# A new order for the opening, two sums of squares in two parts, g_norm loaded later, one cast behind a copy

## The chip, the core and the metric

The kernel runs on one core of a Trainium2 chip. The metric is the device time of one execution in microseconds; a verdict compares the medians of several executions. TensorE is PE, with its weight loads as PEld; VectorE is DVE, ScalarE is ACT, GpSimd is POOL, and SyncE is SP, which issues most of the DMAs.

## The reference

Linear attention without softmax, an RMS norm over each head, then two layers over 4608 tokens of 512 numbers, all in float32:

```python
kv = np.einsum('bhsd,bhse->bhde', k, v)            # 8 batches, 8 heads, 576 x 64
out = np.einsum('bhsd,bhde->bhse', q, kv)
rms = np.sqrt(np.mean(out * out, axis=-1, keepdims=True) + 1e-06)
x = out / rms * g_norm                              # -> 4608 tokens x 512
h = x @ w_in                                        # 2048
x = (np.maximum(h, 0) + np.log1p(np.exp(-np.abs(h)))) @ w_out
h = np.maximum(np.maximum(x @ w1, x @ w2), x @ w3)  # 768
y = h @ w_out2
```

## The kernel before

Tokens lie along the free dimension, and are worked on in five passes of 2 x 456 or 2 x 464. A float32 product is made of three float32r products (high part with high, high with low, low with high), so each operand of the layers is split in two: a cast to the high part, and a subtraction for the low part. Passes 1 to 4 multiply 2 x 2 blocks in Strassen's way with seven products (numbered 1 to 7 in the code); pass 0 multiplies plainly, while the weights arrive, are converted, split and written back to DRAM for the later passes.

The opening is the work ahead of and at the start of pass 0. It is written out as a list, `OPENING`, of steps with indices and an option (an engine a, v or p for ACT, DVE, POOL, or a PSUM tag X, Y, W, at, cv). Eight pairs of heads, numbered 0 to 7 (four pairs for each of two halves of 456 tokens), go through it. For pair k: `LP.k` loads k, v and q on the SP queue (v of pairs 0 to 2 on ACT's), `mm.k` makes k^T v (the first with some idle products, `warm`, between), `ev.k` copies it out of PSUM, `o.k` multiplies q by it, `sq.k` squares the result on ACT, `ss.k` sums the squares over a head with a product by a block of ones, `rs.k` makes the root, `t.k`, `r1.k`, `r2.k`, `r3.k` refine and scale it (r1 uses g_norm as `gcol0`), `xh.k` and `xl.k` split the result. For the weights, `LW.g.i` loads raw numbers, `ra`, `rb` (ACT) and `ja`, `jb` (DVE) convert them, `wc` and `wl` split them, `s1` to `s4` and `cc`, `cl` make and split the sums for the later passes, and `SA`, `SB`, `SC` write parts back. `H.g.i.k` is a plain product of twelve matmuls for half k of the tokens; it needs four split pairs (0 to 3 for k = 0, 4 to 7 for k = 1), the split block `wl.g.i` and a free PSUM bank, and `sp`, `hc`, `hl` take it out through softplus and split it. After the list come the products for g = 8 and 9 (called Xx, Yx in the rows).

What sets the order: for times below `PIN` every engine issues its instructions in the order of the list (`pinned` queues each behind the last one of its engine), so an instruction that waits holds up everything behind it on that engine. The PSUM tags have 2 banks for X, Y and at, and 1 for W and cv. A bank of `o.k` is free after `r1.k`, one of `ss.k` after `r2.k`, one of `H` after `hl`. `load_gain` loads g_norm with a DMA on the SP queue and scales it with two DVE instructions; it is queued at `OPEN - 38.7`, ahead of the list. Raw loads of the weights that follow the list are tied to the last steps `jb` (`before` keeps their times).

In the passes 1 to 4, `combine` makes and splits the inputs of the seven products; its steps 1, 3, 4, 5 make those of products 5 and 6, 7, 4 and 3. `combine_x2` does it for the second layer's results, whose products (`run_group`, bank X for products 1, 6, 7, 4) follow; `sums` copies bank X out on ACT after products 1, 6 and 7 (`copy`). A product that goes on in bank X waits for that copy.

Of the kernel before, what the change touches and what calls it, by code (L numbers as in the profile page):

```python
# [9 lines left out]
F32R = mybir.dt.float32r  # L10
# [5 lines left out]
B, H, S, D = 8, 8, 576, 64  # L16
# [47 lines left out]
BANK = {1: "X", 6: "X", 7: "X", 4: "X", 5: "Y", 3: "Y", 2: "W"}

# [2 lines left out]
def kernel(  # L68
# [12 lines left out]
    nc = tc.nc  # L81
# [23 lines left out]
    def psum(tag, name):  # L105
        return ps.tile([P, 512], F32, tag=tag, bufs=PS_BUFS[tag], name=name)
# [4 lines left out]
    def ctile(name, n, dtype=F32):  # L111
        return wide(cp, "c", 10, name, n, dtype)
# [67 lines left out]
    def at(t, fn, *args):  # L180
        events.append((t, len(events), fn, args))
# [286 lines left out]
    qs, o_t, sq_t, ss_t, og_t, ra_t = {}, {}, {}, {}, {}, {}  # L468
# [118 lines left out]
    def square32(a, n, p):  # L587
# [126 lines left out]
    def run_pass(pas, base):  # L714
# [37 lines left out]
        start = {name: base + 7 * i for i, name in enumerate(order)}  # L752
# [43 lines left out]
        for fp in range(8):  # L796
            t = start[f"H{fp}"]
# [19 lines left out]
        for n in range(4):  # L817
            if pas == 0:
                for q in range(2):
                    t = start[f"X{n}{q}"]  # L820
# [10 lines left out]
            for q in range(2):  # L831
                t = start[f"X{n}{q}"]
# [150 lines left out]
        t = base3 + 2.05  # L983
# [42 lines left out]
    by = {"a": nc.scalar, "v": nc.vector, "p": nc.gpsimd}  # L1026
# [18 lines left out]
    def low(eng, hi, lo, src):  # L1045
        sub(eng, lo, src, hi.bitcast(F32))
# [14 lines left out]
    def pair(f):  # L1061
        return lambda k, *opt: f(k // NP * n0, n0, k % NP, *opt)
# [4 lines left out]
    def plus(g, i, k):  # L1067
# [162 lines left out]
```

## Time and profile before

| | |
|---|---|
| time, median of 3 runs (1357.93 to 1359.16) | 1359.15 us |
| the profiled execution, its own time | 1356.8 us |
| its span | 1355.0 us |
| PE busy | 1346.9 us (99%) |
| PEld busy | 1197.5 us (88%) |
| DVE, ACT, POOL busy | 821.7, 734.9, 650.2 us |

The profiled execution took 1.8 us more than its span, and 2.35 us less than the median. In the rows below, a time at the left is the start in us from the start of the span, and the next number is how long the instruction, or a run of like ones (x4), took. Brackets tell how long the engine's queue idled before it, and what ended that. L12 is line 12 of the kernel. A float32 matmul shows as two instructions, a float32r one as one; each has one weight load.

### The profile page before, as it was taken

The numbers are of one execution on the slowest core, as the hardware profiler recorded it, in microseconds if no ns is written. First come the engines' busy times: TensorE is split into PE (matmuls) and PEld (weight loads), VectorE is DVE, ScalarE is ACT, GpSimd is POOL, SyncE is SP. The second block draws the span as 40 slices with busy tenths as digits, with TensorE's granted clock in tenths as the row PEclk, the third lists the DMA queues.
The fourth block names the chain that finished last, engine by engine and source line by source line (L and its number), as shares of the span: only waits on it lengthen the run. The fifth ranks groups of instructions, "written<-read, shape, count | busy, mean of one in ns | idle before, by whom it ended". The sixth has DMA issues, their size and how long they took to land.

```text
span 1355.0 us, 20402 instructions
## 1 busy us (share of the span) xinstructions
PE 1346.9 (99%) x6956; PEld 1197.5 (88%) x6956; DVE 821.7 (61%) x1301; ACT 734.9 (54%) x1426; POOL 650.2 (48%) x612
## 2 busy tenths in 40 slices
PE   9999999999999999999999999999999999999998
PEld 6889999999888888888888888888888889998897
DVE  6856758883555767734556676445667754457444
ACT  6776657773755366446444664554356546443332
POOL 6866545665645635345335344444434444336320
PEclk9999999999999999999999999999999999999999
DMA  8799789777999686586678756766766576675765
GB/s 297 243 326 347 261 299 346 255 255 260 319 333 319 230 318 220 182 314 204 211 236 273 244 190 209 270 208 208 247 196 215 166 282 219 216 217 187 228 199 172
DMA packets 135543, 336.12 MB, mean 248 GB/s; under 512 B 14608, under 2 KB 41104, under 8 KB 135440
## 3 DMA queue, kind: packets, MB, share of 16 engines
q1 hardware_dynamic: 134864, 333.90, 74.1%
q8 instruction: 56, 0.92, 0.3%
q10 hardware_dynamic: 576, 0.92, 0.2%
q14 instruction: 47, 0.39, 0.1%
HBM read 269.35 MB, written 65.40 MB: 247 GB/s over the span
## 4 chain that ended last, share of the span: by engine, by line
PE 96%; DMA 2%; ACT 1%; DVE 1%; issue 0%; SPq 0%; ACTq 0%; DVEq 0%
PE Xo L155 6%; PE Xo L157 6%; PE Xo L156 6%; PE Xx L157 5%; PE Xx L155 5%; PE Xx L156 5%; PE Xh L155 5%; PE Xh L157 5%; PE Xh L156 5%; PE Yo L155 3%; PE Yo L156 3%; PE Yo L157 3%; PE Yx L155 3%; PE Yx L156 3%; PE Yx L157 3%; PE Yh L155 3%
## 5 line engine op out<-in xcount | busy, mean ns | idle before, releaser
L145 POOL TENSOR_TENSOR lo<-e,hi 128x464 fp32r<-128x464 f32 (+1 forms) x160 | 188.4, 1211 | 176.0 <-ACT hi L139 169.1
L139 ACT CAST hi<-t 128x464 fp32r<-128x464 f32 (+1 forms) x120 | 65.6, 546 | 125.2 <-DVE e L151 55.4
L155 PE MATMUL Xo<-hi,u 128*128 128x464 f32 (+1 forms) x296 | 110.8, 375 | 0.5 <-ACT m L139 0.4
L156 PE MATMUL Xo<-lo,u 128*128 128x464 f32 (+1 forms) x296 | 109.8, 371 | 0.0
L157 PE MATMUL Xo<-hi,u 128*128 128x464 f32 (+1 forms) x296 | 109.7, 371 | 0.0
L155 PE MATMUL Xh<-hi,u 128*128 128x464 f32 (+1 forms) x266 | 99.3, 373 | 1.0 <-DVE lo L151 0.9
L148 DVE TENSOR_TENSOR x<-x,Xx 128x464 f32<-128x464 f32 (+1 forms) x104 | 65.5, 632 | 56.2 <-PE Xx L157 55.8
L157 PE MATMUL Xh<-hi,u 128*128 128x464 f32 (+1 forms) x266 | 98.8, 371 | 0.0
L156 PE MATMUL Xh<-lo,u 128*128 128x464 f32 (+1 forms) x266 | 98.6, 371 | 0.0
L139 ACT CAST hi<-e 128x464 fp32r<-128x464 f32 (+1 forms) x160 | 86.0, 581 | 20.5 <-PE Yx L156 17.1
L139 ACT COPY m<-Xo 128x464 f32<-128x464 f32 (+1 forms) x108 | 58.5, 547 | 69.7 <-PE Xo L157 67.2
L145 DVE TENSOR_TENSOR lo<-t,hi 128x464 fp32r<-128x464 f32 (+1 forms) x120 | 75.8, 636 | 32.5 <-ACT hi L139 30.1
L155 PE MATMUL Xx<-hi,u 128*128 128x464 f32 (+1 forms) x256 | 95.2, 372 | 0.0
L157 PE MATMUL Xx<-hi,u 128*128 128x464 f32 (+1 forms) x256 | 95.0, 371 | 0.0
L156 PE MATMUL Xx<-lo,u 128*128 128x464 f32 (+1 forms) x256 | 94.8, 370 | 0.0
L151 POOL TENSOR_TENSOR e<-e 128x464 f32<-128x464 f32 (+1 forms) x32 | 38.1, 1190 | 106.9 <-DVE t L151 89.6
L145 POOL TENSOR_TENSOR lo<-m,hi 128x464 fp32r<-128x464 f32 (+1 forms) x40 | 47.8, 1212 | 74.4 <-ACT hi L139 74.4
L145 POOL TENSOR_TENSOR u<-sw,u 128x256 fp32r<-128x256 f32 (+1 forms) x67 | 67.5, 1022 | 33.0 <-ACT u L139 31.2
L139 ACT CAST u<-sw 128x512 fp32r<-128x512 f32 (+1 forms) x120 | 63.0, 541 | 35.6 <-POOL sw L151 17.9
L151 POOL TENSOR_TENSOR sw<-sw 128x256 f32<-128x256 f32 x84 | 66.5, 794 | 23.5 <-DVE sw L280 19.3
L148 DVE TENSOR_TENSOR Wh<-h,Wh 128x464 f32<-128x464 f32 (+1 forms) x32 | 20.6, 644 | 92.6 <-PE Wh L157 77.6
L663 POOL TENSOR_TENSOR og<-og,r 128x464 f32<-128x464 f32 (+1 forms) x32 | 40.4, 1262 | 69.5 <-DVE r L659 42.8
(260 smaller groups left out, 4102.8 us busy)
## 6 DMA issues: line engine op xcount, KB each, us to landing
u<-wd SPq DMA_DIRECT2D x241, 512.0 KB, 4.6
ux<-wd SPq DMA_DIRECT2D x99, 512.0 KB, 3.6
wd<-u SPq DMA_DIRECT2D x161, 256.0 KB, 4.8
u<-wd SPq DMA_DIRECT2D x104, 256.0 KB, 4.1
raw<-in_w_out_dram SPq DMA_DIRECT2D x22, 512.0 KB, 4.7
raw<-in_w_dram SPq DMA_DIRECT2D x18, 512.0 KB, 5.4
raw<-in_w_in_dram SPq DMA_DIRECT2D x16, 512.0 KB, 5.5
wd<-ahead SPq DMA_DIRECT2D x32, 256.0 KB, 5.8
```

Of the source, the lines that this page charges most:

```text
L139: nc.scalar.copy(hi, src)
L145: eng_lo.tensor_tensor(out=lo, in0=src, in1=hi.bitcast(F32), op=ALU.subtract)
L148: eng.tensor_tensor(out=o, in0=a, in1=b, op=ALU.add)
L151: eng.tensor_tensor(out=o, in0=a, in1=b, op=ALU.subtract)
L155: nc.tensor.matmul(acc, wh, xh, start=first, stop=False, skip_group_check=on)
L156: nc.tensor.matmul(acc, wh, xl, start=False, stop=False, skip_group_check=on)
L157: nc.tensor.matmul(acc, wl, xh, start=False, stop=last, skip_group_check=on)
L663: nc.gpsimd.tensor_tensor(out=og, in0=og, in1=r, op=ALU.mult)
```

## The change

- `OPENING` is a new list of the same steps with another order, other engines and other PSUM tags, and with four steps more: `vh.0`, `vl.0`, `vh.1`, `vl.1`, all on POOL. They split the squares of the pairs 0 and 1 into a high and a low float32r part, and `ss.0` and `ss.1` then take two float32r products with `ones` in place of a float32 one with `ones32`.
- `load_gain` is queued at `OPEN + 0.6`, between `LP.2` (`OPEN + 0.5`) and `mm.0` (`OPEN + 0.75`), on SP and on DVE.
- In the passes 2 and 3, for the second half of the columns, step 5 of `combine_x2` (the input of product 3) is traced 3.01 after the products' base time in place of 3.5 before it, with an order edge behind the ACT instruction traced last, which is the copy after product 6.

```diff
--- before.py
+++ after.py
@@ -43,23 +43,24 @@
 ENGINES = tuple(getattr(mybir.EngineType, e) for e in ("PE", "Activation", "DVE", "Pool", "SP"))
 LEAD = 10
 OPENING = """
-LP.0 LP.1 LP.2 mm.0 ev.0:a o.0:X LW.0.0 mm.1 sq.0 LP.3 ss.0:Y ev.1:a o.1:X rs.0 mm.2 r1.0 t.0:p sq.1 LP.4
-ra.0.0:cv ss.1:Y ev.2:v rb.0.0 r2.0 o.2:X rs.1 ja.0.0 mm.3 LP.5 sq.2 t.1:p r3.0 ss.2:Y ev.3:a r1.1 xh.0 o.3:W
-LP.6 jb.0.0 rs.2 xl.0:p mm.4 sq.3 r2.1 t.2:a r1.2 wc.0.0:p ss.3:Y ev.4:a r2.2 wl.0.0:p mm.5 LW.0.1 rs.3 r3.1
-o.4:X ev.5:a t.3:p LP.7 r1.3 xh.1 o.5:X r3.2 sq.4 xl.1:p mm.6 sq.5 r2.3 xh.2 ss.5:Y ev.6:v rb.0.1 xl.2:p r3.3
-ss.4:Y ra.0.1:cv LW.1.0 o.6:W rs.5 ja.0.1 xh.3 mm.7 t.5:p r1.5 LW.1.1 sq.6 jb.0.1 xl.3:p rs.4 r2.5 LW.2.0 ev.7:a
-r1.4 o.7:X ra.1.0:cv t.4:p r3.5 rb.1.0 ss.6:Y wc.0.1:p sq.7 H.0.0.0:X r2.4 s1.0 rs.6 ja.1.0 ra.1.1:at t.6:p r1.6
-ra.2.0:at wl.0.1:p jb.1.0 cc.0.1:a ss.7:Y rb.2.0 r2.6 LW.2.1 SA.0 wc.1.0:a cl.0.1 ja.2.0 H.0.1.0:Y rs.7 r3.4
-wl.1.0:p xh.5 SB.0 t.7:a jb.2.0 SC.0.1 xh.4 r2.7 LW.8.0 tab wc.2.0:p r1.7 H.1.0.0:Y r3.6 SA.1 ra.2.1:cv wl.2.0:p
-r3.7 sp.0.0.0 xh.6 xl.5:v hc.0.0.0:a xl.4:p H.2.0.0:X xh.7 hl.0.0.0 rb.2.1 xl.7:p s2.0 s3.0 SA.2 xl.6:v sp.0.1.0
-rb.8.0 ja.2.1 s4.0 H.0.0.1:X hc.0.1.0:a jb.2.1 sp.2.0.0 cc.0.2:p rb.1.1 hl.0.1.0 cl.0.2 LW.8.1 hc.2.0.0:a ja.1.1
-H.2.0.1:Y ra.8.0:cv hl.2.0.0 cc.0.0:p sp.0.0.1 ja.8.0 SC.0.2 cl.0.0 sp.1.0.0 jb.1.1 LW.9.0 hc.0.0.1:a hc.1.0.0:v
-ra.8.1:at s1.1 H.1.0.1:X jb.8.0 LW.9.1 wc.1.1:a cc.1.1:a hl.1.0.0 wl.1.1:p SC.0.0 sp.2.0.1 hl.0.0.1 rb.8.1
-cl.1.1 H.0.1.1:X hc.2.0.1:a ja.8.1 sp.1.0.1 s2.1 hl.2.0.1 wc.2.1:a SB.1 jb.8.1 s3.1 hc.1.0.1:a SC.1.1 wl.2.1:v
-wc.8.1:a H.1.1.1:Y s4.1 cc.1.0:a wl.8.1:v sp.0.1.1 cl.1.0 cc.1.2:a hl.1.0.1 hc.0.1.1:a SB.2 cl.1.2 s1.2 s2.2
-s3.2 s4.2 s1.8 s2.8 s3.8 s4.8 H.2.1.0:X hl.0.1.1 sp.1.1.1 SB.8 hc.1.1.1:v SC.1.0 hl.1.1.1 H.1.1.0:X SC.1.2
-sp.2.1.0 ra.9.0:cv rb.9.0 hc.2.1.0:v hl.2.1.0 ja.9.0 jb.9.0 H.2.1.1:X sp.1.1.0 ra.9.1:W wc.8.0:a hc.1.1.0:v
-hl.1.1.0 wl.8.0:v sp.2.1.1 rb.9.1 hc.2.1.1:v hl.2.1.1 ja.9.1 jb.9.1 SA.8
+LP.0 LP.1 LP.2 mm.0 ev.0:v mm.1 LW.0.0 o.0:X ev.1:v LP.3 o.1:X sq.0 mm.2 vh.0:p sq.1 vl.0:p LP.4 rb.0.0 ev.2:a
+vh.1:p ss.0:Y ra.0.0:cv o.2:W vl.1:p rs.0 ja.0.0 LP.5 mm.3 t.0:a r1.0 sq.2 r2.0 ss.1:Y ev.3:a jb.0.0 ss.2:Y rs.1
+LP.6 r3.0 wc.0.0:a o.3:X t.1:a wl.0.0:p r1.1 mm.4 rs.2 r2.1 sq.3 LW.0.1 mm.5 r1.2 t.2:a ss.3:Y ev.4:v xh.0 LP.7
+r3.1 ev.5:a xl.0:p o.4:X rs.3 r2.2 xh.1 o.5:W t.3:p r1.3 sq.4 SA.0 mm.6 r3.2 ra.0.1:cv xl.1:p sq.5 ss.4:Y LW.1.0
+r2.3 xh.2 mm.7 ev.6:v rb.0.1 xl.2:p r3.3 LW.1.1 rs.4 ss.5:Y ev.7:a ja.0.1 t.4:p o.6:X xh.3 r1.4 rs.5 xl.3:p
+o.7:at jb.0.1 ra.1.0:at r1.5 rb.1.0 LW.2.0 s1.0 H.0.0.0:X r2.4 ra.1.1:cv wc.0.1:p ja.1.0 cc.0.1:a t.5:p sq.6
+r3.4 sq.7 cl.0.1 ss.6:Y rb.1.1 jb.1.0 wl.0.1:p xh.4 r2.5 LW.2.1 rs.6 ja.1.1 ss.7:Y ra.2.0:at wc.1.0:p r1.6
+SC.0.1 t.6:a xl.4:p jb.1.1 H.0.1.0:X rs.7 SB.0 r2.6 wc.1.1:a wl.1.0:p LW.8.0 r1.7 t.7:a tab r3.6 wl.1.1:p
+H.1.0.0:Y r3.5 xh.6 SA.1 s1.1 sp.0.0.0 r2.7 xh.5 xl.6:p r3.7 cc.1.1:a SB.1 H.1.1.0:Y hc.0.0.0:a xh.7 xl.5:p
+hl.0.0.0 sp.0.1.0 xl.7:v sp.1.0.0 s2.1 ra.2.1:cv hc.0.1.0:v H.0.1.1:X cl.1.1 hc.1.0.0:a hl.0.1.0 rb.2.0 s3.1
+hl.1.0.0 rb.8.0 ja.2.0 s2.0 rb.2.1 SC.1.1 H.0.0.1:X jb.2.0 s4.1 cc.1.0:a ja.2.1 LW.8.1 sp.0.1.1 cl.1.0 cc.1.2:a
+jb.2.1 ra.8.0:at hc.0.1.1:v LW.9.0 H.1.1.1:Y cl.1.2 sp.1.1.0 ja.8.0 wc.2.0:a s3.0 hl.0.1.1 sp.0.0.1 SC.1.0 s1.2
+hc.1.1.0:a wl.2.0:v ra.8.1:cv s4.0 H.1.0.1:X SC.1.2 hl.1.1.0 rb.8.1 cc.0.0:p jb.8.0 rb.9.0 cl.0.0 SA.2 ja.8.1
+cc.0.2:a hc.0.0.1:a jb.8.1 H.2.0.0:Y sp.1.1.1 wc.2.1:p LW.9.1 hl.0.0.1 wc.8.1:a s1.8 wl.2.1:v sp.1.0.1 cl.0.2
+SC.0.0 hc.1.1.1:a wl.8.1:v hc.1.0.1:a H.2.0.1:X s2.2 sp.2.0.0 hl.1.0.1 s2.8 ra.9.0:cv SB.2 hl.1.1.1 s3.2
+ra.9.1:at SC.0.2 ja.9.0 hc.2.0.0:a s3.8 SB.8 H.2.1.0:X jb.9.0 rb.9.1 s4.2 sp.2.0.1 hl.2.0.0 s4.8 hc.2.0.1:a
+ja.9.1 wc.8.0:p hl.2.0.1 H.2.1.1:Y sp.2.1.0 wl.8.0:p jb.9.1 hc.2.1.0:v hl.2.1.0 sp.2.1.1 SA.8 hc.2.1.1:v
+hl.2.1.1
 """.split()
 BANK = {1: "X", 6: "X", 7: "X", 4: "X", 5: "Y", 3: "Y", 2: "W"}
 
@@ -590,7 +591,21 @@
         nc.scalar.activation(sq_t[a, p], o, AF.Square)
         og_t[a, p] = o
 
+    def square_hi(a, n, p, eng):
+        sh = ctile("sh", n, F32R)
+        cast(eng, sh, sq_t[a, p])
+        sq_t[a, p] = (sq_t[a, p], sh)
+
+    def square_lo(a, n, p, eng):
+        sq, sh = sq_t[a, p]
+        sl = ctile("sl", n, F32R)
+        low(eng, sh, sl, sq)
+        sq_t[a, p] = (sh, sl)
+
     def ssq_mm32(a, n, p, tag):
+        if isinstance(sq_t[a, p], tuple):
+            ssq_mm(a, n, p, tag)
+            return
         ss_t[a, p] = psum(tag, "ss")[:, 0:n]
         nc.tensor.matmul(ss_t[a, p], ones32, sq_t.pop((a, p)), start=True, stop=True)
 
@@ -852,10 +867,18 @@
         def combine_x2(q, steps):
             combine(xc_tile, R2, q, [x2[q, w] for w in TILES], steps, "at", (1, 2) if q else ())
 
+        def combine_behind(q, steps):
+            traced = reversed(nc.cur_bb.bb.instructions)
+            with tc.issue_after(next(i for i in traced if i.engine is mybir.EngineType.Activation)):
+                combine_x2(q, steps)
+
         for q in range(2 if pas else 0):
             for s, m in ((0, 2), (2, 4)):
                 at(start[f"X3{q}"] + SLOT[m] + 0.45, combine_x2, q, (s,))
-            at(start[f"X3{q}"] + (12.5, 10.5)[q], combine_x2, q, (1, 3, 4, 5))
+            late = q and pas in (2, 3)
+            at(start[f"X3{q}"] + (12.5, 10.5)[q], combine_x2, q, (1, 3, 4) if late else (1, 3, 4, 5))
+            if late:
+                at(start[f"X3{q}"] + 17.01, combine_behind, q, (5,))
         mx, R3 = {}, {}
 
         def h2_done(fp, j, w, src):
@@ -1011,7 +1034,7 @@
     def first_table():
         tables.update(set=NORM_SET, load=nc.scalar.preload_act_table_set(NORM_SET).ins)
 
-    at(OPEN - 38.7, load_gain)
+    at(OPEN + 0.6, load_gain)
     at(OPEN - 38.6, first_table)
     for b in range(2):
         at(OPEN - 50, kv_zero, b)
@@ -1074,6 +1097,8 @@
         "ev": lambda k, eng: kv_evict32(*divmod(k, NP), by[eng]),
         "o": pair(out_mm32),
         "sq": pair(square32),
+        "vh": pair(lambda a, n, p, eng: square_hi(a, n, p, by[eng])),
+        "vl": pair(lambda a, n, p, eng: square_lo(a, n, p, by[eng])),
         "ss": pair(ssq_mm32),
         "rs": pair(root),
         "t": pair(lambda a, n, p, eng: root_square(a, n, p, by[eng])),
```

## Rows read from the trace of the kernel before

**Rows 1.** Window: PE, PEld, DVE, ACT, POOL busy; clock, DMA share, GB/s

```profile
16.00:27.00 11.00, 10.70 (x107) 6.69 (x105) 9.66 (x16) 9.57 (x22) 9.44 (x9) 1.00 0.86 327
```

**Rows 2.** Timeline of PE, the start of the opening

```profile
2.04 2.93 PE L554 MATMUL warm<-kv 128*128 128x128 f32 x12 [2.04 <-DVE kv L535]
4.76 1.06 PE L545 MATMUL kvps<-v,k 128*128 128x128 f32 x4
...
7.59 1.03 PE L584 MATMUL o<-qraw,kv 128*128 128x456 f32 x2
8.55 0.95 PE L513 MATMUL kvps<-v,k 128*64 128x64 f32 x20
9.43 1.03 PE L595 MATMUL ss<-sq,ones 128*128 128x456 f32 x2
10.29 0.93 PE L584 MATMUL o<-qraw,kv 128*128 128x456 f32 x2
```

**Rows 3.** Timeline of PEld (weight loads), the H products and what follows

```profile
30.57 0.19 PEld L155 LDWEIGHTS Yh<-hi,u 128*128 128x128 f32 x1 [0.56 <-DVE t L618]
...
33.62 0.19 PEld L155 LDWEIGHTS Yh<-hi,u 128*128 128x128 f32 x1 [0.66 <-DVE t L618]
...
41.57 0.19 PEld L155 LDWEIGHTS Yh<-hi,u 128*128 128x128 f32 x1 [0.61 <-DVE lo L151]
41.68 0.19 PEld L156 LDWEIGHTS Yh<-lo,u 128*128 128x128 f32 x1
...
46.93 0.19 PEld L155 LDWEIGHTS Xh<-hi,u 128*128 128x128 f32 x1 [0.53 <-DVE lo L151]
...
53.06 0.19 PEld L155 LDWEIGHTS Xh<-hi,u 128*128 128x128 f32 x1 [1.27 <-ACT u L139]
...
60.45 0.19 PEld L155 LDWEIGHTS Xx<-hi,u 128*128 128x128 f32 x1
...
71.27 0.19 PEld L157 LDWEIGHTS Xx<-hi,u 128*128 128x128 f32 x1 [0.43 <-DVE u L145]
```

**Rows 4.** Timeline of SP, the DMA issue behind pair 2

```profile
6.60 0.33 SPq L257 DMA_DIRECT2D raw<-in_w_in_dram  x1
```

**Rows 5.** Waits of SP, 0:10 us: total, times, longest

```profile
SPq L257 <- DMA qraw<-in_qt_dram: 1.7, 1, 1.7
```

**Rows 6.** DMA issues, 0:14 us: count, KB, median us to landing

```profile
qraw<-in_qt_dram SPq DMA_DIRECT2D x6, 228.0 KB, 5.3
...
raw<-in_w_in_dram SPq DMA_DIRECT2D x1, 512.0 KB, 5.0
...
gcol<-in_gn_dram SPq DMA_DIRECT2D x1, 0.5 KB, 2.2
```

**Rows 7.** Timeline of DVE, g_norm's scaling and a copy out of PSUM

```profile
3.00 0.15 DVE L1008 TENSOR_SCALAR gcol<-gcol 128x1 f32<-128x1 f32 x1 [1.02 <-DMA gcol<-in_gn_dram]
...
12.15 0.46 DVE L141 COPY kv<-kvps 64x64 f32<-64x64 f32 x2 [0.22 <-PE kvps L513]
```

**Rows 8.** POOL by line and form, 7:62: count, busy us, mean ns

```profile
L151 POOL TENSOR_TENSOR lo<-og,hi 128x456 fp32r<-128x456 f32 x6 | 7.7, 1276 | 2.2 <-ACT hi L139 2.1
...
L141 POOL CAST u<-sw 128x512 fp32r<-128x512 f32 x4 | 2.9, 712 | 0.0
```

**Rows 9.** Timeline of ACT in pass 2, around the copies of Xo

```profile
735.57 0.58 ACT L139 CAST hi<-x 128x464 fp32r<-128x464 f32 x1
736.18 0.55 ACT L139 COPY m<-Xo 128x464 f32<-128x464 f32 x1
```

**Rows 10.** Timeline of PEld, second layer, passes 2 and 3

```profile
736.77 0.19 PEld L155 LDWEIGHTS Xo<-hi,u 128*128 128x128 f32 x1 [0.50 <-ACT m L139]
...
742.46 0.19 PEld L155 LDWEIGHTS Yo<-hi,u 128*128 128x128 f32 x1
...
999.78 0.19 PEld L155 LDWEIGHTS Xo<-hi,u 128*128 128x128 f32 x1 [0.29 <-ACT m L139]
```

**Rows 11.** Timeline of POOL in pass 2, low parts of the inputs

```profile
734.14 3.47 POOL L145 TENSOR_TENSOR lo<-x,hi 128x464 fp32r<-128x464 f32 x3 [1.13 <-ACT hi L139]
```


## The prediction

> **What bounds the kernel now.** I read the busy shares first: PE is busy 99% of the span, so only time in which PE's stream stands still can be won, and it has to be looked for in the weight loads, since matmul ends are modelled. A float32r product of 456 columns takes 0.207 us from load to load ((60.45 - 53.06 + 0.1) / 36 for three H products in a row), and where a load waits, the brackets show it; the load after it follows 0.11 instead of 0.21 later, so a bracket costs PE its figure less about 0.11 [rows 3]. From 30.57 to 60.45 four brackets cost 0.55 + 0.50 + 0.42 + 1.16 = 2.6, and one at 71.27 costs 0.3 [rows 3]. Behind that only two more carry anything: 0.50 in pass 2 and 0.29 in pass 3, both on ACT's copy of bank X [rows 10].
>
> Ahead of 30.57 there is hardly a gap: per pair, o takes 0.86 to 0.96, mm 0.88 and the float32 sum 0.86 [rows 2]. From the first o (7.59) to the product at 30.57 are 22.98 us; in them lie 8 o (8 x 0.87), 7 mm (7 x 0.88), 8 sums (8 x 0.86) and one H (12 x 0.207), together 22.5. The start is bound by PE, with DVE just behind it (9.66 busy of 11 us from 16 to 27, ACT 9.57, POOL 9.44) [rows 1].
>
> **Sums in two parts.** A float32 sum of 0.86 becomes two products of 0.207: -0.45 each, -0.9 for two. The price is two POOL steps before each sum: a cast (0.71 for 512 columns in the nearest row) and a subtraction (1.28) [rows 8]. Four of them are 4.0 us of POOL, at a time when nothing else is in its list. For pair 1 other products cover the latency; for pair 0 they do not: PE has only o.1 and mm.2 between o.0 and ss.0 (0.86 + 0.88 = 1.74), against a square on ACT (taken as the 0.58 of a like cast [rows 9]), cast and subtraction, 0.58 + 0.71 + 1.28 and some 0.2 for handing over = 2.77. PE waits 1.0 (0.3 if the cast takes 0.4 and the subtraction 1.0; 1.5 if both are a fifth longer).
>
> **g_norm later.** The one issue that SP saves at the head (0.33 for a load [rows 4]) moves no product, since the first ones follow the idle ones without a gap. What it is moved behind decides. On SP it now stands where the raw weights' load stood; that one waited 1.7 us for an earlier q to land and was issued at 6.60 [rows 4, 5]. On DVE its two scalings (0.15 each [rows 7]) now stand ahead of ev.0 and ev.1, which the new list gives to DVE, and behind these stand ja.0.0 and r1.0. So o.0 waits for g_norm, which it doesn't use. When does g_norm land? Alone it took 2.2 us; in this stretch a q of 228 KB takes 5.3, and the raw load of 512 KB, issued at 6.60, took 5.0 [rows 6]. Transfers land in the order of issue: 512 KB at about 400 GB/s are 1.3 us, so the raw load's turn came at 11.6 - 1.3 = 10.3. That is where I put g_norm: 10.3, with bounds 6.2 + 2.2 = 8.4 (issued 0.4 earlier, and not held up) and 11.0. I take 10.3, as the raw load had the very same place in the queue. Then 0.35 for the scalings, 0.46 for the copy [rows 7], 0.1 for handing over: o.0 starts at 11.2. PE, which now makes mm.1 first (7.59 to 8.47), waits 2.7 (bounds 0.9 and 3.4).
>
> **The rest of the new list.** To the second H product (H.0.1.0) PE has 22.5 - 0.9 of work, 2.7 + 1.0 of the waits above, and a wait of 1.0 near the end: ss.7 needs the Y bank that r2.5 frees, which hangs on t.5, fourth in a row of POOL steps, and H.0.1.0 the X bank that r1.6 frees. DVE, nearly full, starts its conversions and refinements only once g_norm is there (bounds 0 and 1.6, against 0.5 in all now). 7.59 + 21.6 + 3.7 + 1.0 = 33.9, where it was 30.57. The other way round the old waits behind it go: they are DVE's and ACT's, each 0.4 to 1.2 long, and PE arrives 3.3 later while DVE's work moves by less; the new list also makes the g = 2 products last, and reuses a bank only after two other products. 33.9 + 11 x 2.48 = 61.2, against 60.45: **+0.8** (bounds: -1.4 with the low ends of the waits, +2.0 with the high ones and 0.5 of waits left).
>
> The wait at 71.27 is for a block whose conversion queues behind a raw load tied to the last jb steps. In the old list jb.9.1 is DVE's last step; in the new one four DVE steps come after it, so these loads leave some 2 to 4 us sooner. That wait goes: **-0.3** (0 to -0.4). SA.0 now stands ahead of LW.1.0 on SP: 512 KB, 1.3 us later for LW.1.0 and LW.1.1. H.1.0.0 comes 2.5 us after H.0.1.0, which covers it; without that cover it costs up to 1.0, within the bounds.
>
> **The cast behind the copy.** In pass 2 the cast of product 3's input (735.57, 0.58) runs directly ahead of the copy of Xo (736.18 to 736.73), and PE's load comes at 736.77 [rows 9, 10]. With the cast behind the copy, the copy starts about 0.6 sooner, more than PE's loss of 0.50 - 0.11; the same in pass 3, 0.29 - 0.11. The moved cast delays its low part on POOL, the last of three up to 737.61 [rows 11], by some 0.4; the next product into Yo comes at 742.46 [rows 10], so that is covered. **-0.6** (bounds +0.2, if the cast then delays a later copy, and -0.8).
>
> **Sum.** +0.8 - 0.3 - 0.6 = -0.1 on the profiled execution's span of 1355.0 (1356.8 with what lies around it). Its time lies 2.35 below the median of the runs, so I set the change against the median: 1359.15 - 0.1, forecast 1359.0. A measurement of this kernel tells about 0.2%, 2.7 us, from no change: the forecast is the same.
>
> **Rivals.** (1) DVE isn't held by g_norm, because it lands early, about 8.4. Against it stands every landing in this stretch at 4 to 5 us after issue. Of the 2.7 not waited only some 1.2 come back, since DVE's 9.66 of 11 is the next bound: 1357.8. (2) The list does all it could: the front costs no more than pair 0's 1.0, no wait is left behind it, 0.5 + 2.6 + 0.3 of old waits go, the sums give 0.9 and the copies 0.6: -3.9, and so 1355.2. For it: 3.4 of waits are really there to be won. Against it: DVE's load, and g_norm. [...] (4) The cast isn't late, or ACT orders otherwise, so that passes 2 and 3 give nothing: 1359.6.
>
> **How the numbers follow.** Forecast 0.57, rival 1 0.17, rival 2 0.12, rival 3 0.09, rival 4 0.05. Faster by over 0.2%: rival 2 and the edge of rival 1, 0.13. Slower: rival 3 and 0.02 of the forecast's upper end, 0.11. The same: 0.76. The range leaves out most of rivals 2 and 3: 1356.2 to 1361.5. The forecast's own bounds (-1.4 - 0.4 - 0.8 and +2.0 + 0 + 0.2, so 1356.6 to 1361.4) lie inside it.
>
> **What would show it.** DVE's scaling of g_norm at about 10.3 and o.0 at about 11.2; ss.0 behind its low part on POOL by 1.0, two weight loads of 0.21 for it; H.0.1.0 near 34, and from there to the first Xx no bracket above 0.2, that Xx near 61.2; none at its second group; in the passes 2 and 3 the copy ahead of the cast and no bracket on Xo. I am wrong if g_norm lands before 8.5, if the products after the pause step at half rate, or if the H products still wait, which would say that DVE moved as far as PE.

## The result, and the profile after

| | before | after |
|---|---|---|
| median of 5 runs, taken together | 1358.03 us (1357.63 to 1359.16) | 1365.52 us (1364.75 to 1366.88) |
| profiled execution, its span | 1356.8, 1355.0 us | 1365.52, 1363.7 us |
| ratio, 95% interval | | 1.0053 (1.0042 to 1.0065) |

The changed kernel is slower by 7.5 us. The forecast of 1359.0 and its range up to 1361.5 missed it. Where the time goes is read by setting the start of the same product of PE in both traces side by side (all times in us):

| product that starts in before at | 63.1 | 100.2 | 137.1 | 145.2 | 175.0 | 725.2 | 745.2 | 1350.0 |
|---|---|---|---|---|---|---|---|---|
| later in after by | 4.45 | 4.41 | 6.44 | 7.26 | 8.99 | 9.12 | 8.76 | 8.73 |

So there are two losses of about the same size, 4.4 in the opening and 4.6 in pass 0 between 100 and 175 us, and a small gain in pass 2. The 4.4 is measured against one execution of before with a quick opening: at 100.2 us three other executions with the old list (with g_norm late, with the cast moved, and with ACT in the order of the code, all below) stand 1.22, 1.12 and 0.50 later than it. The table gives the places of the loss, then, and the medians its size.

**The opening.** Timeline of PE in after, the first o products (they answer to [rows 2]; L585 is o, L514 mm, L662 the first part of a sum in two):

```profile
8.14 0.95 PE L514 MATMUL kvps<-v,k 128*64 128x64 f32 x20
11.83 3.41 PE L585 MATMUL o<-qraw,kv 128*128 128x456 f32 x4 [2.74 <-DVE kv L142]
15.16 1.53 PE L514 MATMUL kvps<-v,k 128*64 128x64 f32 x20
16.63 0.75 PE L662 MATMUL ss<-sh,ones 128*128 128x456 f32 x1
```

Timeline of DVE in after (answers to [rows 7]):

```profile
11.07 0.15 DVE L1031 TENSOR_SCALAR gcol<-gcol 128x1 f32<-128x1 f32 x1 [9.08 <-DMA gcol<-in_gn_dram]
...
11.33 0.94 DVE L142 COPY kv<-kvps 64x64 f32<-64x64 f32 x4
```

Timeline of SP in after, the issue of g_norm (in the place of [rows 4]):

```profile
6.70 0.33 SPq L1030 DMA_DIRECT2D gcol<-in_gn_dram  x1
```

DMA issues of after, 0:14 us: count, KB, median us to landing (answers to [rows 6]):

```profile
gcol<-in_gn_dram SPq DMA_DIRECT2D x1, 0.5 KB, 4.3
```

Issued at 6.70 and landed 4.3 later, g_norm lets DVE go at 11.07; the two copies come behind its two scalings, and o.0 starts at 11.83. And o.0 with o.1 then takes 3.33 to the next product (15.16 - 11.83), where two o took 1.72 before; mm.2 takes 1.47 (16.63 - 15.16) where an mm took 0.88. The windows of after say why (PE, PEld, DVE, ACT, POOL busy; granted clock, DMA share, GB/s):

```profile
9.00:11.80 2.80, 0.09 (x4) 0.00 (x0) 0.66 (x4) 0.00 (x0) 0.00 (x0) 0.78 1.02 370
11.80:16.60 4.80, 4.77 (x24) 2.40 (x24) 0.44 (x2) 1.66 (x3) 2.16 (x3) 0.50 1.03 387
16.60:18.00 1.40, 1.40 (x6) 0.95 (x4) 0.26 (x1) 1.22 (x4) 1.24 (x2) 0.71 1.09 414
16.00:27.00 11.00, 11.00 (x111) 7.07 (x108) 8.47 (x15) 9.84 (x24) 6.28 (x7) 0.94 0.84 293
```

Behind the pause from 9.0 to 11.8 the granted clock is 0.50, and 0.71 in the 1.4 us after that: 3.33 + 1.47 - 1.72 - 0.88 = 2.2 us. Before, with no such pause, it is 1.00 in every window up to 24 us. DVE, 9.66 busy from 16 to 27 us before [rows 1], has 8.47 there: it isn't what the opening waits for now. Further on, weight loads in after (PEld, answers to [rows 3]; a sum of squares, the product H.0.1.0, two later H and the first Xx):

```profile
35.10 0.30 PEld L610 LDWEIGHTS ss<-sq,ones 128*128 128x128 f32 x2 [1.07 <-ACT raw L271]
...
36.53 0.19 PEld L156 LDWEIGHTS Xh<-hi,u 128*128 128x128 f32 x1 [1.13 <-POOL u L142]
...
56.81 0.19 PEld L156 LDWEIGHTS Xh<-hi,u 128*128 128x128 f32 x1 [0.57 <-DVE lo L152]
...
59.83 0.19 PEld L156 LDWEIGHTS Xh<-hi,u 128*128 128x128 f32 x1 [0.65 <-POOL sw L149]
...
65.19 0.19 PEld L156 LDWEIGHTS Xx<-hi,u 128*128 128x128 f32 x1 [0.54 <-POOL u L152]
```

**Pass 0, behind the list.** Before, PE waited for nothing between 100 and 175 us. Waits of PEld in after, 100:175 us (total, times, longest):

```profile
PEld Yx L156 <- DVE lo L146: 3.3, 3, 1.7
PEld Xh L156 <- DVE lo L146: 1.3, 2, 1.0
PEld Yh L156 <- DVE lo L146: 0.9, 1, 0.9
PEld Xx L156 <- DVE lo L146: 0.3, 1, 0.3
```

The longest of them, at 171.70, can be followed back through the timelines of after. PEld:

```profile
171.70 0.19 PEld L156 LDWEIGHTS Yx<-hi,u 128*128 128x128 f32 x1 [1.68 <-DVE lo L146]
```

DVE, the low part that this load waits for, and ahead of it a low part of weight sums:

```profile
165.77 0.90 DVE L146 TENSOR_TENSOR u<-sw,u 128x512 fp32r<-128x512 f32 x1
...
171.01 0.63 DVE L146 TENSOR_TENSOR lo<-Yh,hi 128x456 fp32r<-128x456 f32 x1 [3.79 <-ACT hi L140]
```

ACT:

```profile
169.17 0.41 ACT L140 CAST u<-sw 128x256 fp32r<-128x256 f32 x1 [3.42 <-POOL sw L152]
169.48 0.53 ACT L176 ACTIVATE Yh<-Yh 128x456 f32<-128x456 f32 x1
169.95 0.60 ACT L140 CAST u<-sw 128x512 fp32r<-128x512 f32 x1
170.45 0.53 ACT L140 CAST hi<-Yh 128x456 fp32r<-128x456 f32 x1
```

POOL:

```profile
166.75 0.75 POOL L149 TENSOR_TENSOR sw<-sw 128x256 f32<-128x256 f32 x1 [0.63 <-DVE u L146]
167.58 1.55 POOL L152 TENSOR_TENSOR sw<-sw 128x256 f32<-128x256 f32 x2
```

ACT stands 3.42 at a cast of weight sums (for the later passes), which POOL has ready only at 169.13 (167.58 + 1.55): its step at 166.75 waited for DVE's of 165.77. The softplus of Yh, whose last product's weights were loaded at 167.35 (PE made that product from 167.56 to 167.93), and the cast of its high part stand behind that cast, DVE's low part behind these, and PE behind that. (The other waits were not followed back in this way; ACT's waits for POOL's sums in total, shown below, go with them.) The order in which these steps stand in ACT's queue is not written in the code: behind the list, for some two thirds of pass 0, only SP's order is given, and the framework's scheduler chooses that of ACT, DVE and POOL. Between 75 and 175 us the traces show PE's products in one and the same order in before and after, and those three engines' steps in two different ones. It is the list that changed them: where only g_norm or only the copy's cast was changed (two of the experiments below) they have before's order. In the kernel before the same kinds of steps stand so on ACT (timeline of before):

```profile
155.77 0.55 ACT L175 ACTIVATE Yh<-Yh 128x456 f32<-128x456 f32 x1
156.24 0.40 ACT L139 CAST u<-sw 128x256 fp32r<-128x256 f32 x1
156.53 0.55 ACT L139 CAST hi<-Yh 128x456 fp32r<-128x456 f32 x1
158.98 0.62 ACT L139 CAST u<-sw 128x512 fp32r<-128x512 f32 x1 [1.91 <-POOL sw L151]
```

There the cast that waits stands behind the high part of Yh, and its 1.91 cost PE nothing.

**Passes 2 and 3.** Timeline of ACT in after, the copy of Xo and the cast now behind it (answers to [rows 9]):

```profile
744.73 0.55 ACT L140 COPY m<-Xo 128x464 f32<-128x464 f32 x1
745.17 0.58 ACT L140 CAST hi<-x 128x464 fp32r<-128x464 f32 x1
```

Weight loads behind these copies in passes 2 and 3 of after (answer to [rows 10]):

```profile
745.33 0.19 PEld L156 LDWEIGHTS Xo<-hi,u 128*128 128x128 f32 x1 [0.24 <-ACT m L140]
...
1008.30 0.19 PEld L156 LDWEIGHTS Xo<-hi,u 128*128 128x128 f32 x1 [0.24 <-ACT m L140]
```

The order is as meant; the brackets fall from 0.50 (736.77) and 0.29 (999.78) to 0.24 each (745.33 and 1008.30), the same as behind the second copy of pass 3 (1010.51), ahead of which ACT had idled 1.19. That second copy had a bracket before as well, 0.44 at 1002.00, and the one of pass 2 fell from 0.34 (738.99) to 0.28 (747.55); the prediction's rows leave these two out. The shift falls from 9.12 to 8.76 in pass 2.

### The profile page after: what moved, and what is told of

It reads as the page before. It is cut to its first block, busy times and chain, and to the rows that moved or that the text cites. A ratio compares the mean times of both kernels' runs of the same rounds, so it can differ in the third digit from the quotient of the medians.

```text
span 1363.7 us, 20381 instructions
## 1 busy us (share of the span) xinstructions
PE 1350.3 (99%) x6956; PEld 1198.6 (88%) x6956; DVE 818.8 (60%) x1303; ACT 735.5 (54%) x1426; POOL 652.4 (48%) x614
## 4 chain that ended last, share of the span: by engine, by line
PE 91%; DMA 2%; DVE 2%; ACT 2%; POOL 1%; issue 1%; SPq 0%; DVEq 0%; POOLq 0%; ACTq 0%
PE Xo L156 6%; PE Xo L158 6%; PE Xo L157 6%; PE Xx L156 5%; PE Xx L158 5%; PE Xx L157 5%; PE Xh L156 4%; PE Xh L157 4%; PE Xh L158 4%; PE Yo L156 3%; PE Yo L157 3%; PE Yo L158 3%; PE Yx L156 3%; PE Yx L157 3%; PE Yx L158 3%; PE Yh L158 2%
## 5 line engine op out<-in xcount | busy, mean ns | idle before, releaser
L156 PE MATMUL Xh<-hi,u 128*128 128x464 f32 (+1 forms) x262 | 97.8, 373 | 1.5 <-DVE lo L146 0.6
L158 PE MATMUL Xh<-hi,u 128*128 128x464 f32 (+1 forms) x262 | 97.2, 371 | 0.0
L152 POOL TENSOR_TENSOR sw<-sw 128x256 f32<-128x256 f32 x84 | 67.6, 807 | 33.9 <-DVE sw L281 30.0
```

The source lines that it names most:

```text
L152: eng.tensor_tensor(out=o, in0=a, in1=b, op=ALU.subtract)
L156: nc.tensor.matmul(acc, wh, xh, start=first, stop=False, skip_group_check=on)
L158: nc.tensor.matmul(acc, wl, xh, start=False, stop=last, skip_group_check=on)
```

## The experiments

Each was timed in several rounds beside the kernel before; a ratio is to that one, with its 95% interval.

**The front by itself.** g_norm early again:

```diff
-    at(OPEN + 0.6, load_gain)
+    at(OPEN - 38.7, load_gain)
```

> The changed kernel with g_norm loaded ahead of the list again, as before; nothing else. Theory: of the 7.5 us lost, some 4.4 are lost up to the first Xx product (it came 4.45 later than before) because DVE's first steps stood behind g_norm (PE idle from 8.97 to 11.83) and the products after that pause ran at half the clock; a separate 4.6 are lost in pass 0 behind the list (shift from +4.4 at 100 us to +9.0 at 170 us), where the order on ACT, DVE and POOL came out otherwise. By it o.0 starts near 9.0, no stretch of the opening shows a granted clock below 1, the first Xx comes near 60.5 to 61, and the waits of PE between 110 and 172 stay: 1361.5 to 1362. Rival A: pass 0's waits are only the late opening handed on (its loads and conversions come later against PE): then they go as well, and the time is about 1357.5. Rival B: the clock falls here too, as mm.1 is followed by a shorter pause: about 1363.5.

1365.39 us, ratio 1.0056 (1.0042 to 1.0070). The opening did what the theory said: first o at 9.29, no clock below 1, same product at 63 us later by 1.02 in place of 4.45. But the median missed the expectation, it is that of the changed kernel: between 100 and 175 us this execution lost 5.1 (1.57 to 6.64), with PE waiting at the same products. So the late opening isn't what makes pass 0 wait (rival A), and what the opening wins is lost there. Rival B has a part in it: two of the five runs show a mean granted clock of 0.997 and 0.998, and these are the longest, 1366.57 and 1367.08.

The first two copies on ACT in place of DVE, g_norm late:

```diff
-... mm.0 ev.0:v mm.1 LW.0.0 o.0:X ev.1:v ...
+... mm.0 ev.0:a mm.1 LW.0.0 o.0:X ev.1:a ...
```

> The changed kernel with g_norm late as in it, but the first two copies out of PSUM (ev.0, ev.1) on ACT in place of DVE, so that neither o.0 nor o.1 stands behind g_norm; DVE's own first steps (ja.0.0, r1.0) still do. Theory: it is the place of the two copies on DVE, not the late g_norm as such, that stops PE: o.0 near 9.0, full clock, the time within 0.7 of the version with g_norm loaded early, so 1361.5 to 1362.5. Rival: g_norm's load being late holds r1.0 and the refinements behind it too, and PE waits for them later on: 1363 or more.

1364.38 us, 1.0051 (1.0038 to 1.0064), and no clock below 1 in the opening; the product at 63 us 1.53 later. With both copies off DVE, the late g_norm stops nobody at the front. The total is 2 above the expectation, by the same loss in pass 0 (1.33 to 6.72).

The late load in the old list (the same one line as above, the other way round, in the kernel before):

> The kernel before with g_norm loaded at the later place (between LP.2 and mm.0 on SP and DVE); nothing else. In the old list the first two copies out of PSUM are on ACT, and DVE's first step (r1.0, near 11.2) needs g_norm anyway. Theory: the later load by itself costs nothing where no step stands behind it on DVE: 1358.0, within 0.3, no pause of PE and no clock below 1. Rival: the load in the queue of the k, v, q loads delays these or r1.0 and PE follows: 1359 to 1360.

1358.59 us against 1358.17, 1.0002 (0.9993 to 1.0010): as expected, nothing. DVE's scaling came at 11.06 there too, with no step of PE behind it.

**Idle products in the pause.**

```diff
+    at(OPEN + 0.25 * OPENING.index("mm.1") + 0.01, warm, 13)
```

> The changed kernel with 13 idle products of 128 columns more (as those at the very start, into a bank of their own, their result unused) put right behind mm.1, so that PE has something to do while it waits for g_norm and the copy. o.0 still can't start before about 11.8. Theory: the half clock after the pause costs 2.2 to 2.3 us by itself (o.0 and o.1 took 3.34 in place of 1.72, mm.2 1.46 in place of 0.88): with PE busy in the pause the products after it run at full rate, the first Xx comes about 2 sooner than in the changed kernel, and the time is 1363.2 to 1363.8. Rival: the half-rate products ran in time that DVE or ACT would have taken anyway, so that the full clock gives nothing: 1365.5.

1366.10 us, 1.0061 (1.0049 to 1.0074). o.0 at 12.21 at full rate (13.84 - 12.21 = 1.63 for two o, granted clock 1.00), the product at 63 us 1.5 earlier than in after (2.93 against 4.45), and nothing of it left at 175 us (8.60). Inconclusive on the price of the clock, as pass 0 hid it; it is taken up again below.

**The cast behind the copy alone**, in the kernel before (the diff of `combine_x2` as above):

> The kernel before with the third part of the change alone: in passes 2 and 3 the cast of product 3's input behind the copy of bank Xo. Theory: PE's waits of 0.50 and 0.29 on that copy go, 0.4 and 0.2 of them are won (in the changed kernel the shift against before fell by 0.36 in pass 2 and by 0.3 in pass 3): 0.6 below the kernel before, 1357.6 if that one gives 1358.2. Rival: the moved cast makes another copy or a low part late, and nothing is won: 1358.2.

1357.69 us against 1358.32, 0.9997 (0.9989 to 1.0006). The trace shows the shift fall by 0.36 at pass 2 (1.51 to 1.15) and 0.15 at pass 3 (1.15 to 1.00): 0.5 for the expected 0.6, below what the times can tell.

**ACT in the order of the code behind the list.** One branch more (it also takes the place of the branch that ties the first steps behind the list to the list's last ones), in the kernel before, in the new list with g_norm early, and in the changed kernel:

```diff
+        elif t < third - 2:
+            pinned(fn, args, (mybir.EngineType.SP, mybir.EngineType.Activation))
```

> The kernel before with one thing added: from the end of the list to two thirds of pass 0 ACT too issues in the order in which the program traces its steps (so far only SP did; the order of ACT, DVE and POOL was chosen by the framework's scheduler). The order that results on ACT, DVE and POOL is another one than before's, and the same as in the next kernel but one, whatever the list. Both theories leave the time open within 1355 to 1364; it is the base for the next two.

> The new list with g_norm loaded early (that version alone took 1365.4 against 1358.2 of before) and ACT's order behind the list kept as traced; behind the list ACT, DVE and POOL then have the order of the kernel before with the same thing added. Theory: the 5.8 us that the new list loses between 100 and 172 us come from the other order that the scheduler chose behind it, and go if the order is the same: within 1.0 of that kernel (opening +0.9, copies -0.5). Rival: they come from the new list itself, which leaves conversions of weights behind it later than the old one, so that ACT, DVE and POOL are short of time in pass 0 in whatever order: 4 to 7 above that kernel.

> The changed kernel (g_norm late) with ACT's order behind the list kept as traced: beside the one with g_norm early it prices the front by itself. Theory: the 2.7 of waiting and the half clock behind it cost 3.4 at 63 us (first Xx +4.45 against +1.02), and where pass 0 has no chain of its own that binds, they come through to the end: 3.0 to 3.5 above the version with g_norm early and the same order. Rival: pass 0 swallows it, as it did without the kept order (both then took 1365.4 to 1365.5): within 1.

1361.69 (1.0027, 1.0019 to 1.0036), 1364.05 (1.0044, 1.0030 to 1.0057) and 1364.58 us (1.0046, 1.0033 to 1.0058). In all three the loss between 100 and 175 us is gone: the shifts go from 0.50 to 0.45, 1.14 to 1.02, 4.19 to 4.01. But this order has a loss of its own between 175 and 300 us, 3.3, 3.7 and 4.3, in the old list as well. And the medians of the second and third stand 2.4 above the first and 0.5 apart, for the expected 1.0 and 3.0 to 3.5 (in the profiled executions, 1361.52, 1361.95 and 1365.12, it is 0.4 and 3.2). What makes the second that slow is not shown. In its profiled execution, the shortest of its five, PE's clock fell with g_norm early as well, behind two short waits that come with the sums in two parts. Timeline of PE, new list with g_norm early and ACT so ordered (L663 is the second part of a sum):

```profile
11.80 0.48 PE L662 MATMUL ss<-sh,ones 128*128 128x456 f32 x1
12.73 0.48 PE L663 MATMUL ss<-sl,ones 128*128 128x456 f32 x1 [0.45 <-POOL sl L152]
13.87 1.43 PE L585 MATMUL o<-qraw,kv 128*128 128x456 f32 x2 [0.66 <-ACT kv L140]
```

Its windows from 14 to 18 us:

```profile
14.00:16.00 2.00, 2.00 (x16) 0.94 (x18) 1.59 (x3) 1.94 (x4) 0.42 (x1) 0.59 1.04 394
16.00:18.00 2.00, 2.00 (x15) 1.56 (x12) 1.48 (x3) 0.63 (x4) 0.00 (x0) 0.55 1.06 393
```

So the order does decide where pass 0 loses, but this experiment puts another order in place of before's. The next ones give before's own.

**List and order crossed.** Behind the list the 174, 123 and 94 instructions of ACT, DVE and POOL of pass 0's first 110 plan units are queued one behind the other, as they stand in the other kernel (the numbers count them as the code makes them):

```diff
+QUEUED = {
+    "Activation": """
+0 1 2 5 13 3 14 19 20 4 31 32 6 7 10 11 8 9 16 12 18 21 15 22 23 24 25 26 28 17 39 40 27 35 48 49 29 38 30 41 33
...
+    queued = mybir.DependencyInfo(mybir.DependencyClass.NoSync, mybir.DependencyReason.DATA)
+    for e, ins in kept.items():
+        order = [ins[int(n)] for n in QUEUED[e].split()]
+        for i, j in zip(order, order[1:]):
+            tc.add_manual_dep(j, i.name, queued, reason="issue_after")
```

New list, g_norm early, before's order:

> The new list with g_norm loaded early, and behind the list the very order of the kernel before: the 174 instructions of ACT, 123 of DVE and 94 of POOL that belong to the first 110 plan units of pass 0 are queued one behind the other as they stand in the kernel before. Theory: the order behind the list costs the new list 5 to 6 us between 100 and 172 us, by itself. With before's order the shift against the kernel before stays where it is at the first Xx product (about +1, as other executions of the old list show it too), passes 2 and 3 give 0.6 back: 1357.5 to 1358.5 where the clock holds, 1 to 3 more in executions in which it falls at 14 to 18 us. Rival A: the new list leaves the conversions later, and the order only spreads that: 1361 to 1364. Rival B: PE's clock falls in most executions, and that is what the median shows: 1360 to 1361.

The changed kernel with before's order:

> The changed kernel as it is (g_norm late) with the order of the kernel before behind the list, made in the same way. Theory: its front (first Xx +4.4) comes through undiminished, pass 0 adds nothing, passes 2 and 3 give 0.6 back: 3.0 to 3.8 above the kernel before, 1361.2 to 1362.0, and 3.5 below the changed kernel. Rival: the order is not the cause and pass 0 still loses its 4.6: 1365.5.

The kernel before with the changed kernel's order:

> The crossed case: the old list and all else of the kernel before, with the order of the changed kernel on ACT, DVE and POOL behind the list, queued in the same way. Theory: the order alone costs what the changed kernel lost there: PE waits at the same products for DVE's low parts between 100 and 175 us, and the time is 4 to 6 above before, 1362 to 1364. Rival: the order costs only after the new list: 1358.2 within 1.

| list | order behind it | us | ratio | later at 100.2, 175.0 |
|---|---|---|---|---|
| new, g_norm late | its own (after) | 1365.52 | 1.0053 (1.0042 to 1.0065) | 4.41, 8.99 |
| new, g_norm late | before's | 1359.97 | 1.0009 (1.0000 to 1.0018) | 4.08, 3.92 |
| new, g_norm early | its own | 1365.39 | 1.0056 (1.0042 to 1.0070) | 1.57, 6.64 |
| new, g_norm early | before's | 1358.25 | 1.0001 (0.9992 to 1.0010) | 3.40, 3.25 |
| old | the changed kernel's | 1364.89 | 1.0050 (1.0037 to 1.0062) | 4.71, 8.60 |

The shifts are those of the one profiled execution of each; in the fourth row it was the longest of eleven, 1360.30, with a slow opening (last section). With before's order the new list loses nothing in pass 0; with the new order the old list loses as much as the changed kernel did, some of it earlier (2.1 later at 71.3 us, 4.7 at 100.2). The order alone is worth 5.6 (after against the second row), 7.1 and 6.8 us. The prices do not simply add: g_norm late costs 1.7 with before's order and 0.3 with the new one (7.5 and 7.2 above their kernels before). Two sizes were missed: the changed kernel with before's order came out better than expected (1361.2 to 1362.0), the old list with the new order 0.9 worse (1362 to 1364). Waits of ACT, 60:180 us, for POOL's weight sums (total, times, longest), first of after, then of the changed kernel with before's order, then of the kernel before with the new order (the kernel before itself has 16.1, 10, 4.3):

```profile
ACT u L140 <- POOL sw L152: 26.0, 15, 3.5
```

```profile
ACT u L161 <- POOL sw L173: 16.3, 10, 4.4
```

```profile
ACT u L160 <- POOL sw L172: 26.1, 14, 3.7
```

And PEld's waits in 100:175 us in the last of these, where the changed kernel with before's order has none:

```profile
PEld Yx L176 <- DVE lo L166: 3.0, 3, 1.5
PEld Xh L176 <- DVE lo L166: 2.3, 2, 1.7
PEld Yh L176 <- DVE lo L166: 0.9, 1, 0.9
```

**Without the sums in two parts.** As the fourth row, with `vh` and `vl` of pairs 0 and 1 left out of the list:

> The new list with g_norm early, before's order behind it, and the first two pairs' squares summed in one float32 product each as before (steps vh and vl left out of the list). It prices the sums in two parts. Theory: these save 0.9 of PE's time but bring the two waits at 12.7 and 13.9 (0.45 and 0.66, about 1.6 of standing still) behind which PE's clock fell in the profiled execution of one kernel with this list; without them no stretch is below a clock of 1, and the median is the same as or up to 1.5 below that of the kernel with the sums in two parts. Rival: the two-part sums are a plain gain of 0.9: 0.9 above it.

1356.66 us against 1358.11, 0.9991 (0.9983 to 1.0000): 1.6 below the fourth row, and the only version whose interval lies below the kernel before, just so, by less than the 0.2% that counts here. PE goes from the first o to ss.2 without a wait or a clock below 1.

**What in the order costs it.** The old list with the new order on ACT alone, and on ACT and DVE:

> The kernel before with the changed kernel's order behind the list on ACT alone; DVE and POOL keep before's. Theory: ACT's queue carries it: there casts of weight sums, which wait for POOL, now stand ahead of the softplus steps and casts that PE's next product needs (ACT waited 26 us for POOL's sums between 60 and 180 us, where it was 16). Most of the 6.8 comes with ACT alone: 1362.5 to 1365. Rival: PE's waits end on DVE's low parts, and it takes DVE's order as well: 1358 to 1360.

> As the one before, with the changed kernel's order on ACT and DVE, and before's on POOL. Theory: POOL's order adds nothing, as PE waits for hardly any step of POOL: 1364 to 1365.5, what all three orders gave (1364.9). Rival: POOL's sums, on which ACT's casts wait, are a part of it: 1362 or less.

1377.18 us (1.0141, 1.0125 to 1.0157) and 1370.37 us (1.0085, 1.0071 to 1.0099): 18.8 and 12.0 above the kernel before, where all three gave 6.8. Neither theory had that. ACT's new order alone does harm, and DVE's and POOL's new orders take some of it away again, 6.8 and 5.2. But an order on ACT that does not fit the other two queues may be a loss of its own (on ACT alone the mean granted clock is 0.994 to 0.998 too), so these two runs do not show how much of the 6.8 is ACT's. Waits of PEld with the new order on ACT alone, 60:200 us (ACT's for POOL's sums are 28.2 there):

```profile
PEld Yx L176 <- DVE lo L166: 8.7, 3, 3.8
...
PEld Yh L176 <- DVE lo L166: 3.0, 1, 3.0
```

DVE's or POOL's new order alone was not run.

**The clock once more.** The idle products in the pause, now with before's order:

> The changed kernel with before's order behind the list (1359.97) and 13 idle products more right behind mm.1, so that PE is busy while it waits for g_norm and the copy. Theory: the half clock behind that pause is most of what the late g_norm costs (1359.97 against 1358.25 with g_norm early); with the clock kept up the products catch up while DVE and ACT are behind: 1358.2 to 1359.0. Rival: it is the wait itself, and the clock costs nothing: 1360.0 or, as the idle products can delay mm.2 a little, 1360.2.

1359.13 us against 1358.38, 1.0002 (0.9993 to 1.0011); without the idle products 1359.97 against 1358.11. The difference of 1.1 goes the way of the theory (1359.13 is 0.1 above what it expected), and is smaller than the two intervals together. The clock is plainer: ten of the eleven executions without the idle products have a mean granted clock of 0.997 to 0.999, all eleven with them 1.000. So is the trace of PE, o.0 and o.1 at full rate (13.96 - 12.34 = 1.62) and mm.2 in 0.88:

```profile
9.33 3.17 PE L576 MATMUL warm<-kv 128*128 128x128 f32 x26
12.34 1.70 PE L606 MATMUL o<-qraw,kv 128*128 128x456 f32 x4
13.96 0.95 PE L535 MATMUL kvps<-v,k 128*64 128x64 f32 x20
14.84 0.48 PE L683 MATMUL ss<-sh,ones 128*128 128x456 f32 x1
```

## Why the prediction was wrong

From the runs, each against the kernel before that was timed beside it: order behind the list 5.6; g_norm late 1.7 (1.86 - 0.14); sums in two parts 1.6 (0.14 + 1.45); cast behind the copy -0.6; and so -0.8 for the rest of the list (-1.45 + 0.6). Together 7.5. Each but the first is uncertain by 1 us or more, and they hold in the sequence in which they were taken (the order first, then g_norm, then the sums).

- *For pass 0 the sum ended at 71 us.* This is the step that failed. It took the work behind the list as it was and set only the wait at 71.27 against it. But the new list changed the order that the scheduler chose on ACT, DVE and POOL for the next 100 us, and 5.6 of the 7.5 lie there. With before's order the changed kernel takes 1359.97, inside the range and 1.0 above the forecast. Part of that is luck: it is 1.9 above its kernel before, where -0.1 was forecast, and the forecast stood on a median of three, 1359.15, that all later medians of the kernel before (1358.0 to 1358.4) lie under.
- *g_norm.* DVE's place in front of the copies, SP's issue behind an earlier q and the place in the queue of loads were right: 6.70 for 6.60, scaling at 11.07 for 10.3, o.0 at 11.83 for 11.2, PE idle for 2.74 where 2.7 was forecast. The landing lies at the upper bound given, 11.0. What the turn in the queue was reckoned from, the traces show: the loads that SP issued in the first 14 us landed in the order of issue, in before (the q of 4.44 at 9.5, the raw load of 6.60 at 11.6) as in after (the q of 3.69 at 10.7, g_norm at 11.0, the raw load of 7.07 at 12.2), and before moved 395 GB/s from 5 to 10 us and 393 from 10 to 15.
- *PE's clock.* Rival 3, that the clock falls behind the new pause, happened, together with the forecast and not in its place. No run had shown such a fall when it was given its chance of 0.09; after shows a granted clock of 0.50 for 4.8 us behind a pause of 2.74. It cost 2.2 in the opening of this execution; of that, 1.1 came through to the end with before's order (not clear of noise), and nothing with the new one. The chance was the mistake: the prediction itself put a pause of 2.7 into the opening, and the trace of before, with no pause of that length between its products, could not tell what the clock does behind one.
- *Sums in two parts.* The wait at ss.0 was 0.6 in place of 1.0 (12.83 - 11.89 - 0.31, with g_norm early), as PE takes the high part while POOL makes the low one. By the prediction's estimate of 0.9 that should leave a gain of 0.3. The runs show a loss of 1.6: in one execution the copy behind it came late as well (0.66) and the clock fell behind the two waits; with before's order three of eleven executions have a mean granted clock below 1, and none of the eleven without the two parts. How the 1.6 is divided between these stays open.
- *The rest of the list.* H.0.1.0 came at 36.5 for 33.9: 0.6 by g_norm, 2.2 by the clock. Nearer to it, the wait put at 1.0 shows as three brackets, 0.48 (at 33.73), 1.07 and 1.13, while the 1.0 at ss.0 was not there in this execution. Of the waits behind it, which should all go, 0.57, 0.65 and 0.54 are there. The one at 71.27 went as forecast.
- *The cast behind the copy.* Right in kind, 0.5 for 0.6: a copy that is not late still leaves a bracket of 0.24. The reading that only two brackets follow behind 71 us was wrong: before has more of them, 0.40 at 478.54 and 0.44 at 1002.00 among them; the second of these fell with the change too.

## What to carry to other kernels

Where a stretch is ordered by hand and the rest by a scheduler, a change of the stretch is a change of all that follows: set the issue orders of both programs side by side, engine by engine, past the edit, before the edit is costed, and keep the old order in an experiment so that the two can be priced apart. A step that waits for another engine and serves a later pass must not stand ahead of the steps that the next product needs. And what PE is spared in products is not won if it brings waits: here two sums in two parts, estimated to spare PE 0.9, made the kernel 1.6 slower, the latter uncertain by about 1.

## What the runs showed of the hardware

- PE's idle time of 2.74 us was followed by a granted clock of 0.50 for 4.8 us; filled with idle products, it was not (1.00 from 8 to 20 us, new list and before's order). Two waits of 0.45 and 0.66 with 0.5 of work between them were followed by 0.59 and 0.55 in one execution (windows above). Executions of one kernel differ: the mean granted clock of the five of after was 0.997 to 1.000, and the one with 1.000 was the longest. What makes them differ no run shows.
- The granted clock of a window doesn't tell all: in the profiled execution of the new list with g_norm early and before's order (1360.3, its median is 1358.25) o.0 and o.1 go at half rate (3.34 for the two, 14.19 - 10.85, where before took 1.72) while the windows from 8 to 16 us show 1.00. No pause of PE stands ahead of it, which was busy for 3.89 of the 4 us from 4 to 8: the four idle products at 8.24 already took 1.15 to the next product, where they took 0.59 before (7.00 to 7.59 [rows 2]). Timeline of PE:

```profile
8.24 1.22 PE L576 MATMUL warm<-kv 128*128 128x128 f32 x4
9.39 1.53 PE L535 MATMUL kvps<-v,k 128*64 128x64 f32 x20
10.85 3.41 PE L606 MATMUL o<-qraw,kv 128*128 128x456 f32 x4
14.19 1.32 PE L535 MATMUL kvps<-v,k 128*64 128x64 f32 x20
```

- On ACT a ready step waited behind one that wasn't: ACT stood 3.42 us at a cast, the last 1.2 of them (169.17 - 167.93) with the softplus of Yh ready to go, and issued it behind that cast, at 169.48.
- A DMA of 0.5 KB took 2.2 us from issue to landing with nothing ahead of it [rows 6], and 4.3 behind the loads of k, v and q.
